# Routed attention and MLP-mixer on one core: small TensorE products regrouped within each pair of heads

## The chip, the cores and the metric

The kernel runs on one core of one Trainium2 chip. The metric is the device time of one execution in microseconds (us). The kernel before took 915.86 us, the median of 3 runs from 915.76 to 915.94. A "pair" below is two heads of one batch, which the kernel handles together. There are 4 batches of 8 heads, so 16 pairs.

## The reference

An attention whose mask comes from clusters feeds a token mixer and a channel mixer. Cut to what matters:

```python
# q, k, v: (4, 8, 768, 64) float32; centroids: (8, 16, 64)
q_assign = argmax(normalized(q) @ normalized(centroids).T)       # one of 16 clusters
k_assign = argmax(normalized(k) @ normalized(centroids).T)
mask   = q_assign[:, :, :, None] == k_assign[:, :, None, :]
scores = where(mask, q @ k.T / 8, -1e9)
attn   = exp(scores - scores.max(-1)); attn /= attn.sum(-1) + 1e-9
x      = (attn @ v) with the heads side by side                   # (4, 768, 512)
h      = relu(x.T @ w_tok1) @ w_tok2                              # 768 -> 256 -> 768
u      = x + h.T
out    = u + relu(u @ w_ch1) @ w_ch2                              # 512 -> 1536 -> 512
```

## The kernel before

For each pair `g` the kernel turns queries and keys (VectorE, tile `qkT`), multiplies them with the centroids (tile `pr`, TensorE), and takes the best cluster as a one-hot code (tiles `sim`, `mx`, `oh`, VectorE). It turns the codes on TensorE (tile `po`) and copies them out of the accumulators (PSUM) to tile `ohT`. The keys' copy is scaled so that the product of two codes is 0 in the same cluster and a huge negative number in another. This product is the mask. Scores are computed as keys by queries, one chunk of 128 keys by 384 queries (half of the queries) for two heads side by side in the array. First comes the mask in bfloat16 (`sc<-ohT`), then q times k in float32 on top of it (`sc<-qkT`). A step `m` takes three chunks, so a pair has four steps, numbered `s` = 0 to 3.

```python
    ps_w  = pool("ps_w", 1, space=PSUM)              # one bank: small products
    ps_av = pool("ps_av", 1, space=PSUM)             # one bank
    ps_sc = pool("ps_sc", NG, ps_sc_stack, space=PSUM)   # NG = 3 buffers of two banks
    ...
    work = pool("work", 7, attention)                # exponentials, tile ex
    sums = pool("sums", 2, attention)
    ...
    def scores(m):
        g, qh, j0 = split(m)                         # pair, half of the queries, first chunk
        scs = [ps_sc.tile([P, 2, 512], F32, tag="sc", name="sc") for _ in range(NG)]
        for src, start in ((st["ohT"], True), (st["T"], False)):     # masks, then products
            for i in range(NG):
                for h in range(2):
                    rows = slice(h * D, (h + 1) * D)
                    nc.tensor.matmul(
                        scs[i][:, h, 0:HS], lhsT=src[rows, 1, j0 + i], rhs=src[rows, 0, js],
                        start=start, stop=not start)
        for i in range(NG):
            ex = work.tile([P, 2, HS], F32, name="ex")
            nc.scalar.activation(out=ex, in_=scs[i][:, :, 0:HS], func=ACT.Exp, scale=SM_SCALE)

    def values(m):       # per chunk and head: av (64 x 384) += v . ex; after six chunks copied to avT
        ...
    def add_up(m):       # VectorE: the exponentials of a half added up, chunk by chunk, in tile sum
        ...
    def half_sums(hi):                               # TensorE: sum over the keys -> den
        den = st["den"] = ps_w.tile([P, 2 * HJ, QP], F32, tag="w", name="den")
        for i in range(NQ):                          # four products, each 32 columns of the array
            nc.tensor.matmul(den[rows], lhsT=ones, rhs=acc[:, :, rows], start=True, stop=True)
    def half_reciprocals(hi):                        # VectorE: den turned (dent), 1 / dent -> rcps
        ...
    def half_turn(hi):                               # TensorE: avT turned back -> px
        px = st["px"] = ps_w.tile([P, HJ, P], F32, tag="w", name="px")
        for i in range(HJ):
            nc.tensor.transpose(out=px[:, i], in_=avT[:, i], identity=ident)
    def half_out(hi):                                # VectorE: px * rcps -> x
        ...
    for m in range(last + 3):                        # last = 64 steps
        g, s = divmod(m, GROUPS)
        more = g < NPAIR - 1
        if half_at(m - 3) is not None: half_out(half_at(m - 3))
        if more and s == 0: turn(g + 1)              # VectorE
        if more and s == 1: route(g + 1)             # VectorE: sim, mx, oh
        if 1 <= m <= last: add_up(m - 1)
        if m < last: scores(m)
        ...                                          # at m == last: other PSUM pools
        if half_at(m - 2) is not None: half_sums(...); half_reciprocals(...)
        if more and s == 2: route_turn(g + 1, 1)     # po of the keys, copied by ScalarE
        if 1 <= m <= last: values(m - 1)
        if half_at(m - 2) is not None: half_turn(half_at(m - 2))
        if more and s == 0: route_products(g + 1)    # pr
        if more and s == 2: route_turn(g + 1, 0)     # po of the queries
        ...                # loads; every third step one piece of the mixers' weights is rounded
        if m >= last:
            for _ in range(3): ends.pop(0)()         # token mixer: tok1, tok2
    ...                                              # channel mixer
```

A half ends at steps `s` = 1 and 3, and its `den` and `px` come two steps later, at `s` = 3 and 1. Each engine works off its own instructions in the order in which they are issued here.

Of the kernel before, what the change touches and what calls it, by code (L numbers as in the profile page):

```python
# [18 lines left out]
P = 128  # L19
# [28 lines left out]
def kernel(  # L48
# [52 lines left out]
    loads = pool("loads", 3, attention)  # L101
    small = pool("small", 2, attention)
    qktp = pool("qktp", 2, attention)
    work = pool("work", 7, attention)
    sums = pool("sums", 2, attention)

    routing = fast.enter_context(ExitStack())
    qkpool = pool("qkpool", 2, routing, side="right")
    rsmall = pool("rsmall", 2, routing, side="right")
    pools = {}  # L110


# [3 lines left out]
    cnT = const.tile([P, H * C], F32, name="cnT")  # L116
    cnd = const.tile([P, NF, 2, C], F32, name="cnd")
    ohs = [rsmall.tile([P, 2, NJ, P], BF16, name=f"oh{i}", bufs=1) for i in range(2)]
    rcps = const.tile([P, 2 * NPAIR, 2, HJ], F32, name="rcps")
    cells = const.tile([P, NPAIR], F32, name="cells")  # L120

    W = {
# [55 lines left out]
    def weight_steps(pool, W, names):  # L178

        def tmp(name, dt, n):
            return pool.tile([P, WMAX], dt, tag=name, name=name)[:, 0:n]

        def load_bits(src, p):  # L190
            n = p["n"] = src.shape[1]
            raw = pool.tile([P, WMAX, 2], U32, tag="raw", name="raw", bufs=3)[:, 0:n]
            nc.sync.dma_start(raw.rearrange("p n two -> p (n two)"), src.bitcast(U32))
            p["lo"], p["hi"] = raw[:, :, 0], raw[:, :, 1]

        def scalar_part(p):

            p["h"] = tmp("wh", U32, p["n"])
            nc.scalar.activation(out=p["h"].bitcast(F32), in_=p["hi"].bitcast(F32), func=ACT.Abs)
            p["up"] = tmp("wup", I32, p["n"])  # L200
            nc.scalar.activation(out=p["up"], in_=p["lo"], func=ACT.Copy, scale=float(2.0**-29))

        def rest(dst, p):

            h = p["h"]
            nc.vector.tensor_scalar(
                out=h.bitcast(F32), in0=h.bitcast(F32), scalar1=TINY, scalar2=HUGE,
                op0=ALU.max, op1=ALU.min,
            )

            nc.vector.tensor_scalar(
                out=h, in0=h, scalar1=0x07FFFFFF, scalar2=3,
                op0=ALU.bitwise_and, op1=ALU.logical_shift_left,
            )
            T = tmp("wT", U32, p["n"])
            nc.vector.scalar_tensor_tensor(  # L216
                out=T, in0=p["hi"], scalar=0xC0000000, in1=h,
                op0=ALU.bitwise_and, op1=ALU.bitwise_or,
            )
            T, up = T.bitcast(I32), p["up"]  # L220
            if len(dst.shape) == 3:
                T, up = (y.rearrange("t (p j) -> t p j", j=NJ) for y in (T, up))
            nc.gpsimd.tensor_tensor(out=dst.bitcast(I32), in0=T, in1=up, op=ALU.add)  # L223

        pieces = list(weight_pieces(W, names))
        parts = [{} for _ in pieces]
        for i in range(len(pieces) + 2):

            def step(i=i):
                if 2 <= i:  # L230
                    rest(pieces[i - 2][0], parts[i - 2])
                if 1 <= i <= len(pieces):
                    scalar_part(parts[i - 1])
                if i < len(pieces):
                    load_bits(pieces[i][1], parts[i])

            yield step
# [50 lines left out]
                in_=st["qk"][:, a].rearrange("p j i d -> p (j i d)"),  # L288
            )

    def wtile(g, shape, dt, name):

        if g == 0:
            return ps_sc.tile(shape, dt, tag="sc", name=name)
        return ps_w.tile(shape, dt, tag="w", name=name)

    def route_products(g, a0=0, a1=2):

        st, f = state[g], g % NF
        pr = wtile(g, [P, a1 - a0, NJ, QP], F32, "pr")  # L300
        for i in range(NQ):
            rows = slice(i * QP, (i + 1) * QP)
            nc.tensor.matmul(  # L303
# [6 lines left out]
    def route(g, a0=0, a1=2):  # L310
# [4 lines left out]
        NR = (a1 - a0) * NJ * 2  # L315
        sc = rsmall.tile([P, NR, C], F32, name="sim")
        nc.vector.transpose(
            out=sc.rearrange("p n c -> p (n c)"), in_=st.pop("pr").rearrange("p a j r -> p (a j r)")
        )
        mx = rsmall.tile([P, NR], F32, name="mx")  # L320
        nc.vector.reduce_max(out=mx, in_=sc, axis=AX.X)
# [4 lines left out]
            op=ALU.is_ge,  # L326
        )

    def route_turn(g, a):

# [3 lines left out]
        st, oh = state[g], ohs[g % 2]  # L336
        if a == 1:
            st["ohT"] = qktp.tile([P, 2, NJ, P], BF16, name="ohT")
        po = wtile(g, [P, NJ, P], BF16, "po")
        for j in range(NJ):  # L340
            nc.tensor.transpose(out=po[:, j], in_=oh[:, a, j], identity=identb)  # L341
        if a == 0:
            if g == 0:
                nc.vector.tensor_copy(out=st["ohT"][:, 0], in_=po)  # L344
            else:
                nc.scalar.copy(out=st["ohT"][:, 0], in_=po)
        else:
            nc.scalar.activation(
                out=st["ohT"][:, 1], in_=po, func=ACT.Copy, scale=BIG, bias=-BIG,
                accum_out=cells[:, g : g + 1],  # L350
            )
# [7 lines left out]
    def scores(m):  # L359
# [1 line left out]
        st = state[g]  # L361
        js = slice(HJ * qh, HJ * qh + HJ)
        scs = [ps_sc.tile([P, 2, 512], F32, tag="sc", name="sc") for _ in range(NG)]
        for src, start in ((st["ohT"], True), (st["T"], False)):
            for i in range(NG):
                for h in range(2):
                    rows = slice(h * D, (h + 1) * D)
                    nc.tensor.matmul(  # L368
                        scs[i][:, h, 0:HS], lhsT=src[rows, 1, j0 + i], rhs=src[rows, 0, js],
                        start=start, stop=not start,  # L370
                    )
        for i in range(NG):
            ex = work.tile([P, 2, HS], F32, name="ex")
            nc.scalar.activation(out=ex, in_=scs[i][:, :, 0:HS], func=ACT.Exp, scale=SM_SCALE)  # L374
# [2 lines left out]
    def add_up(m):  # L377
# [1 line left out]
        st = state[g]  # L379
        e = [st["ex", qh, j0 + i] for i in range(NG)]  # L380
        if j0 == 0:
            acc = st["sum", qh] = sums.tile([P, 2, HS], F32, name="sum")
            nc.vector.tensor_tensor(out=acc, in0=e[0], in1=e[1], op=ALU.add)
            e = e[2:]
        acc = st["sum", qh]
        for ex in e:
            nc.vector.tensor_tensor(out=acc, in0=acc, in1=ex, op=ALU.add)  # L387

    def values(m):
# [9 lines left out]
                    start=(j == 0), stop=(j == NJ - 1),  # L399
                )  # L400
        if j0 == NJ - NG:
            st["avT", qh] = sums.tile([P, HJ, P], F32, name="avT")
            nc.scalar.copy(out=st["avT", qh].rearrange("p j t -> p (j t)"), in_=st.pop("av"))

    def half_sums(hi):

        g, qh = divmod(hi, 2)
        st = state[g]
        acc = st.pop(("sum", qh)).rearrange("p h (j t) -> p (h j) t", j=HJ)
        den = st["den"] = ps_w.tile([P, 2 * HJ, QP], F32, tag="w", name="den")  # L410
        for i in range(NQ):
            rows = slice(i * QP, (i + 1) * QP)
            nc.tensor.matmul(den[rows], lhsT=ones, rhs=acc[:, :, rows], start=True, stop=True)  # L413

    def half_reciprocals(hi):
        g, qh = divmod(hi, 2)
        dt = small.tile([P, 2 * HJ, QP], F32, name="dent")
        nc.vector.transpose(
            out=dt.rearrange("p n r -> p (n r)"),
            in_=state[g].pop("den").rearrange("p n r -> p (n r)"),  # L420
        )
        nc.vector.reciprocal(
            out=rcps[:, hi].rearrange("p h j -> p (h j)"), in_=dt[:, :, 0]
        )

    def half_turn(hi):
        g, qh = divmod(hi, 2)
        st = state[g]
        avT = st.pop(("avT", qh))
        px = st["px"] = ps_w.tile([P, HJ, P], F32, tag="w", name="px")  # L430
        for i in range(HJ):
            nc.tensor.transpose(out=px[:, i], in_=avT[:, i], identity=ident)  # L432

    def half_out(hi):

        g, qh = divmod(hi, 2)
        b, f = divmod(g, NF)
        nc.vector.tensor_tensor(  # L438
            out=xs[b][:, HJ * qh : HJ * qh + HJ, f * P : (f + 1) * P].rearrange(
                "p j (h d) -> p j h d", h=2  # L440
            ),
            in0=state[g].pop("px").rearrange("p j (h d) -> p j h d", h=2),
            in1=rcps[:, hi].rearrange("p h j -> p j h").unsqueeze(3).to_broadcast([P, HJ, 2, D]),
            op=ALU.mult,
        )
        if qh == 1:
# [224 lines left out]
    def fits():  # L671

        inside = const.tile([P, 3, 2 * NPAIR * 2 * HJ], F32, name="inside")
        good = const.tile([P, 3], F32, name="good")
        flat = rcps.rearrange("p n h j -> p (n h j)")
        for i, (limit, op) in enumerate(((LIMIT, ALU.is_le), (1.0 / LIMIT, ALU.is_ge))):
            nc.vector.tensor_scalar(
                out=inside[:, i], in0=flat, scalar1=limit, scalar2=None, op0=op
# [57 lines left out]
    begin()  # L736
    weights = list(weight_steps(stage, W, ("tok1", "tok2", "ch1")))
    last = NPAIR * GROUPS
    HALF = GROUPS // 2
    ends = [lambda t=t: tok1(0, t) for t in range(NT)]  # L740
    for b in range(B):
        if b + 1 < B:
            ends += [lambda b=b, t=t: tok1(b + 1, t) for t in range(NT)]
        ends += [lambda b=b, j=j: tok2(b, j) for j in range(NJ)]

    def half_at(m):

        return m // HALF if 0 <= m < last and m % HALF == HALF - 1 else None

    for m in range(last + 3):  # L750
        g, s = divmod(m, GROUPS)
        more = g < NPAIR - 1
        if half_at(m - 3) is not None:
            half_out(half_at(m - 3))
        if more and s == 0:
            turn(g + 1)
        if more and s == 1:
            route(g + 1)
        if 1 <= m <= last:
            add_up(m - 1)  # L760
        if m < last:
            scores(m)
        if m == last:
            ps_sc_stack.close()
            pools["ps_m"] = pool("ps_m", 2, space=PSUM)
        if half_at(m - 2) is not None:
            half_sums(half_at(m - 2))
            half_reciprocals(half_at(m - 2))
        if more and s == 2:
            route_turn(g + 1, 1)  # L770
        if 1 <= m <= last:
            values(m - 1)
        if half_at(m - 2) is not None:
            half_turn(half_at(m - 2))
        if more and s == 0:
            route_products(g + 1)
        if more and s == 2:
            route_turn(g + 1, 0)
        if s == 1 and g + 2 < NPAIR:
            load(g + 2)  # L780
        if m == last - GROUPS:
# [254 lines left out]
```

## Time and profile before

| What | Value |
|---|---|
| time, median of 3 runs | 915.86 us |
| profiled span | 914.3 us |
| VectorE busy | 507.3 us (55%) |
| ScalarE busy | 303.5 us (33%) |
| GpSimd busy | 45.0 us (5%) |
| weight loads of TensorE | 533.6 us (58%) |
| steps of the attention | first scores at 15.8 us, last `av` product begins at 365.4 us |

The attention is the first two fifths of the span; the token mixer and the channel mixer follow. In the attention the page counts each float32 product as two records of TensorE, the bfloat16 ones as one. A transpose counts as one record. Products on disjoint rows or columns of the array run side by side, so the mean duration of one record (482 ns for `sc<-qkT`) is longer than the time that passes from one to the next of the stream. Stream times are therefore read from the starts of blocks in the timeline. In the timeline a row gives the start, the time from there to the end of the last record of the block, engine and line, output and inputs, the tile of the array with the form of the operands, and the count of records. "128*32" means 128 rows by 32 columns of the array.

### The profile page before, as it was taken

To read this page: it belongs to the slowest core of one execution; us is meant where nothing else is said; L and a number is where in the kernel's file an instruction comes from. 1 tells how busy PE (TensorE), PEld (TensorE's weight loads), DVE (VectorE), ACT (ScalarE), POOL (GpSimd) and SP (SyncE) were. 2 spreads that over 40 slices of the span, in tenths; PEclk is the share of its full clock that TensorE was granted. 3 is DMA by queue.
4 is the path that set the end of the run, shared out by engine and by line. 5 is a ranking of instruction groups with operands and counts; after the bars stand their busy time and mean duration, and the time that the engine had idled before them with its cause. 6 is when DMAs were issued, how large, how long until landed. Compare 5 with 4: busy or idle time off the path is not lost.

```text
span 914.3 us, 11630 instructions
## 1 busy us (share of the span) xinstructions
PE 895.6 (98%) x4594; PEld 533.6 (58%) x4594; DVE 507.3 (55%) x851; ACT 303.5 (33%) x515; POOL 45.0 (5%) x40
## 2 busy tenths in 40 slices
PE   7999999999999999999999899999999999999997
PEld 3444444444444444444458568677686876858676
DVE  5787787787787875577463244333443334433342
ACT  2655565565565654231130121211212012130210
POOL 1000010010010100131000000000000000000000
PEclk9999999999999999999999899999999999999999
DMA  9725426325334100240000001000010000100001
GB/s 154 157 54 107 82 70 109 80 75 99 76 85 89 62 27 1 65 143 1 0 1 1 0 1 47 23 1 1 0 47 24 0 1 12 47 12 1 1 12 61
DMA packets 112830, 41.76 MB, mean 46 GB/s; under 512 B 101632, under 2 KB 105728, under 8 KB 112768
## 3 DMA queue, kind: packets, MB, share of 16 engines
q1 hardware_dynamic: 109632, 40.55, 19.4%
q10 hardware_dynamic: 3136, 0.39, 0.4%
q8 instruction: 38, 0.62, 0.3%
q14 instruction: 24, 0.20, 0.1%
HBM read 34.64 MB, written 6.29 MB: 45 GB/s over the span
## 4 chain that ended last, share of the span: by engine, by line
PE 92%; DVE 5%; DMA 1%; issue 1%; ACT 0%; DVEq 0%
PE sc L368 16%; PE pX L652 14%; PE pX L601 14%; PE av L397 13%; PE pZ L652 7%; PE pZ L601 7%; PE ph L470 5%; PE pu L479 5%; PE pY L652 3%; PE pY L601 3%; PE px L432 2%; DVE sum L387 2%; PE po L341 2%; PE den L413 1%; PE pr L303 1%; PE pt L542 1%
## 5 line engine op out<-in xcount | busy, mean ns | idle before, releaser
L374 ACT ACTIVATE ex<-sc 128x768 f32<-128x768 f32 x192 | 141.8, 812 | 117.5 <-PE sc L368 117.5
L397 PE MATMUL av<-ex,va 128*64 128x384 f32 x768 | 138.0, 494 | 0.0
L387 DVE TENSOR_TENSOR sum<-sum,ex 128x768 f32<-128x768 f32 x128 | 130.1, 1016 | 10.1
L368 PE MATMUL sc<-qkT 64*128 64x384 f32 x768 | 134.3, 482 | 0.0
L368 PEld LDWEIGHTS sc<-qkT 64*128 64x128 f32 x768 | 71.4, 187 | 38.0
L397 PEld LDWEIGHTS av<-ex,va 128*64 128x64 f32 x768 | 49.4, 136 | 66.2 <-issue 59.8
L601 PE MATMUL pX<-uT,wc 128*128 128x384 f32 x192 | 68.8, 495 | 1.6 <-issue 1.6
L609 ACT COPY p<-pX 128x384 f32<-128x384 f32 x24 | 11.4, 475 | 153.1 <-PE pX L601 153.1
L601 PEld LDWEIGHTS pX<-uT,wc 128*128 128x128 f32 x192 | 36.7, 193 | 26.7 <-issue 3.3
L223 POOL TENSOR_TENSOR wc<-wT,wup 128x512 int32<-128x512 int32 x24 | 32.4, 1349 | 251.2 <-DVE wT L216 251.2
L368 PE MATMUL sc<-ohT 64*128 64x384 bf16 x384 | 42.6, 327 | 0.6 <-DVE ohT L344 0.6
L479 PE MATMUL pu<-h,wt 128*128 128x512 f32 x96 | 42.0, 592 | 0.0
L470 PE MATMUL ph<-x,wt 128*128 128x512 f32 x96 | 42.0, 593 | 0.0
L496 DVE TENSOR_TENSOR x<-pX,x 128x256 f32<-128x256 f32 x24 | 10.2, 424 | 55.1 <-PE pX L652 55.1
L496 DVE TENSOR_TENSOR c<-pZ,u 128x384 f32<-128x384 f32 x24 | 13.4, 557 | 46.8 <-PE pZ L601 46.8
L652 PE MATMUL pX<-w2s,hA 128*128 128x256 f32 x144 | 36.4, 390 | 0.5 <-DVE x L496 0.5
L438 DVE TENSOR_TENSOR x<-px,rcps 128x384 f32<-128x384 f32 x32 | 17.8, 556 | 33.5 <-PE px L432 33.5
L496 DVE TENSOR_TENSOR hA<-pY,p 128x384 f32<-128x384 f32 x24 | 13.4, 557 | 40.4 <-PE pY L601 40.4
L652 PE MATMUL pX<-wc,hA 128*128 128x256 f32 x144 | 35.0, 379 | 0.0
L601 PE MATMUL pZ<-uTs,w1s 128*128 128x384 f32 x96 | 35.0, 487 | 0.0
L652 PE MATMUL pX<-w2s,hS 128*128 128x256 f32 x144 | 35.0, 379 | 0.0
L652 PE MATMUL pZ<-wc,hS 128*128 128x256 f32 x144 | 35.0, 379 | 0.0
(115 smaller groups left out, 1227.0 us busy)
## 6 DMA issues: line engine op xcount, KB each, us to landing
raw<-in_moe_w_ch_dram SPq DMA_DIRECT2D x24, 512.0 KB, 3.9
qk<-in_k_dram SPq DMA_DIRECT2D x64, 96.0 KB, 4.4
va<-in_v_dram SPq DMA_DIRECT2D x16, 384.0 KB, 3.3
out_dram<-x SPq DMA_DIRECT2D x24, 256.0 KB, 2.0
qk<-in_q_dram SPq DMA_DIRECT2D x60, 96.0 KB, 3.6
raw<-in_moe_w_tok_dram SPq DMA_DIRECT2D x3, 512.0 KB, 5.8
raw<-in_moe_w_tok_dram SPq DMA_DIRECT2D x4, 384.0 KB, 4.2
qk<-in_q_dram ACTq DMA_DIRECT2D x4, 96.0 KB, 4.8
```

The lines of the kernel that those rows point to most:

```text
L223: nc.gpsimd.tensor_tensor(out=dst.bitcast(I32), in0=T, in1=up, op=ALU.add)
L341: nc.tensor.transpose(out=po[:, j], in_=oh[:, a, j], identity=identb)
L368: nc.tensor.matmul(scs[i][:, h, 0:HS], lhsT=src[rows, 1, j0 + i], rhs=src[rows, 0, js], start=start, stop=not start,)
L374: nc.scalar.activation(out=ex, in_=scs[i][:, :, 0:HS], func=ACT.Exp, scale=SM_SCALE)
L387: nc.vector.tensor_tensor(out=acc, in0=acc, in1=ex, op=ALU.add)
L397: nc.tensor.matmul(st["av"][h * D : (h + 1) * D], lhsT=st["va"][:, h, j], rhs=ex[:, h], start=(j == 0), stop=(j == NJ - 1),)
L432: nc.tensor.transpose(out=px[:, i], in_=avT[:, i], identity=ident)
L470: nc.tensor.matmul(pf, lhsT=W["tok1"][:, j, t * P : (t + 1) * P], rhs=xs[b][:, j], start=(j == 0), stop=(j == NJ - 1),)
L479: nc.tensor.matmul(pu, lhsT=W["tok2"][:, t, j], rhs=h1s[b][:, t], start=(t == 0), stop=(t == NT - 1))
L496: nc.vector.tensor_tensor(out=dst, in0=a, in1=b, op=ALU.add)
L601: nc.tensor.matmul(psum, lhsT=A[a][:, k, c * P : (c + 1) * P], rhs=R[r][:, k], start=start and k == 0, stop=k == 1, skip_group_check=not s ...
L652: nc.tensor.matmul(psum, lhsT=h2[a][:, k, i * P : (i + 1) * P], rhs=Bw[w][:, 3 * part + k], start=start and k == 0, stop=k == 2, skip_grou ...
```

## The change

Three things are done to the attention loop, and buffers are moved to make room for them.

1. **Small products gathered in three places.** The sums of a pair's two halves (`den`) become one product of 384 columns per block of columns instead of two of 192, and stand with the next pair's centroid products (`pr`) after the values of step 1. They share a tile of the score pool, `den` in its first bank and `pr` in its second. Both turns of the codes (`po`) and the first half's turn back (`px`) stand after the values of step 2, the second `px` after those of step 3.
2. **The third chunk's masks behind two chunks' scores.** The new tiles take buffers of the score pool, which the third chunk of the next step takes over. Its masks are now issued after the float32 products of chunks one and two, so that there is time to read the small products out.
3. **Clusters turned ahead of use.** The copies of `ohT` are made before the pair that uses them, after step 2; that of the queries moves from ScalarE to VectorE.

For room, `work` goes from 7 buffers to 6, `rsmall` from 2 to 1, and the temporary `wT` of the weight rounding from 2 to 1; `sum` and `avT` hold a whole pair. The diff, cut to its core:

```diff
-    work = pool("work", 7, attention)
+    work = pool("work", 6, attention)
-    rsmall = pool("rsmall", 2, routing, side="right")
+    rsmall = pool("rsmall", 1, routing, side="right")
 ...
         if a == 0:
-            if g == 0: nc.vector.tensor_copy(out=st["ohT"][:, 0], in_=po)
-            else:      nc.scalar.copy(out=st["ohT"][:, 0], in_=po)
+            nc.vector.tensor_copy(out=st["ohT"][:, 0], in_=po)
 ...
-        for src, start in ((st["ohT"], True), (st["T"], False)):
-            for i in range(NG):
+        for chunks in (range(NG - 1), (NG - 1,)):
+            for src, start in ((st["ohT"], True), (st["T"], False)):
+                for i in chunks:
 ...
-    def half_sums(hi):                    # den: 192 columns, own tile in ps_w
+    def pair_sums(g, den):                # den: 384 columns, tile given
 ...
     for m in range(last + 3):
+        old = g - 1 if m < last else -1
-        if half_at(m - 3) is not None: half_out(half_at(m - 3))
-        if more and s == 1: route(g + 1)
+        if s == 2:
+            if old >= 0: pair_denominators(old)       # VectorE: dent
+            if more:     route(g + 1)                 # VectorE: sim, mx, oh
+            if old >= 0: pair_reciprocals(old)
+        if s == 3 and old >= 0: half_out(old, 0)
+        if s == 0 and old >= 1: half_out(old - 1, 1)
         if more and s == 0: turn(g + 1)
         add_up(m - 1)
         scores(m)
-        if half_at(m - 2) is not None: half_sums(...); half_reciprocals(...)
-        if more and s == 2: route_turn(g + 1, 1)
         values(m - 1)
-        if half_at(m - 2) is not None: half_turn(...)
-        if more and s == 0: route_products(g + 1)
-        if more and s == 2: route_turn(g + 1, 0)
+        if m < last and s == 1:
+            two = ps_sc.tile([P, 2, 512], F32, tag="sc", name="small")
+            if old >= 0: pair_sums(old, two[:, 0, 0:HS])
+            if more:     route_products(g + 1, pr=two[:, 1, 0:HS])
+        if m < last and s == 2:
+            if more:
+                two = ps_sc.tile([P, 2, 1024], BF16, tag="sc", name="po")
+                for a in (1, 0): route_turn(g + 1, a, ...)
+            if old >= 0: half_turn(old, 0, ps_w.tile(...))
+        if m < last and s == 3 and old >= 0:
+            half_turn(old, 1, ps_w.tile(...))
+        # m == last + 1: den, dent, reciprocals and both px of the last pair together
```

More of the change, by code (lines that the diff above doesn't have):

```diff
@@ L118 @@
     ohs = [rsmall.tile([P, 2, NJ, P], BF16, name=f"oh{i}", bufs=1) for i in range(2)]
-    rcps = const.tile([P, 2 * NPAIR, 2, HJ], F32, name="rcps")
+    rcps = const.tile([P, NPAIR, 2, 2, HJ], F32, name="rcps")
     cells = const.tile([P, NPAIR], F32, name="cells")
@@ L187, in tmp @@
         def tmp(name, dt, n):
-            return pool.tile([P, WMAX], dt, tag=name, name=name)[:, 0:n]
+            bufs = 1 if name == "wT" else 2
+            return pool.tile([P, WMAX], dt, tag=name, name=name, bufs=bufs)[:, 0:n]
         def load_bits(src, p):
@@ L289, in turn, with route_products @@
             )
[L291 to L297, printed above, removed]
+    def route_products(g, a0=0, a1=2, pr=None):
         st, f = state[g], g % NF
-        pr = wtile(g, [P, a1 - a0, NJ, QP], F32, "pr")
+        if pr is None:
+            pr = ps_sc.tile([P, (a1 - a0) * NJ * QP], F32, tag="sc", name="pr")
         for i in range(NQ):
@@ L317, in route @@
         nc.vector.transpose(
-            out=sc.rearrange("p n c -> p (n c)"), in_=st.pop("pr").rearrange("p a j r -> p (a j r)")
+            out=sc.rearrange("p n c -> p (n c)"), in_=st.pop("pr")
         )
@@ L327, in route, with route_turn @@
         )
-    def route_turn(g, a):
+    def route_turn(g, a, po=None):
         st, oh = state[g], ohs[g % 2]
@@ L338, in route_turn @@
             st["ohT"] = qktp.tile([P, 2, NJ, P], BF16, name="ohT")
-        po = wtile(g, [P, NJ, P], BF16, "po")
+        if po is None:
+            po = ps_sc.tile([P, NJ, P], BF16, tag="sc", name="po")
         for j in range(NJ):
@@ L342, in route_turn @@
         if a == 0:
[L343 to L346, printed above, removed]
+            nc.vector.tensor_copy(out=st["ohT"][:, 0], in_=po)
         else:
@@ L363, in scores @@
         scs = [ps_sc.tile([P, 2, 512], F32, tag="sc", name="sc") for _ in range(NG)]
-        for src, start in ((st["ohT"], True), (st["T"], False)):
-            for i in range(NG):
[L366 to L371, printed above, removed]
+        for chunks in (range(NG - 1), (NG - 1,)):
+            for src, start in ((st["ohT"], True), (st["T"], False)):
+                for i in chunks:
+                    for h in range(2):
+                        rows = slice(h * D, (h + 1) * D)
+                        nc.tensor.matmul(
+                            scs[i][:, h, 0:HS], lhsT=src[rows, 1, j0 + i], rhs=src[rows, 0, js],
+                            start=start, stop=not start,
+                        )
         for i in range(NG):
@@ L381, in add_up @@
         if j0 == 0:
-            acc = st["sum", qh] = sums.tile([P, 2, HS], F32, name="sum")
+            if qh == 0:
+                st["sum"] = sums.tile([P, 2, 2, HS], F32, name="sum")
+            acc = st["sum"][:, qh]
             nc.vector.tensor_tensor(out=acc, in0=e[0], in1=e[1], op=ALU.add)
             e = e[2:]
-        acc = st["sum", qh]
+        acc = st["sum"][:, qh]
         for ex in e:
@@ L401, in values @@
         if j0 == NJ - NG:
-            st["avT", qh] = sums.tile([P, HJ, P], F32, name="avT")
-            nc.scalar.copy(out=st["avT", qh].rearrange("p j t -> p (j t)"), in_=st.pop("av"))
-    def half_sums(hi):
-        g, qh = divmod(hi, 2)
+            if qh == 0:
+                st["avT"] = sums.tile([P, NJ, P], F32, name="avT")
+            js = slice(HJ * qh, HJ * qh + HJ)
+            nc.scalar.copy(out=st["avT"][:, js].rearrange("p j t -> p (j t)"), in_=st.pop("av"))
+    def pair_sums(g, den):
         st = state[g]
-        acc = st.pop(("sum", qh)).rearrange("p h (j t) -> p (h j) t", j=HJ)
-        den = st["den"] = ps_w.tile([P, 2 * HJ, QP], F32, tag="w", name="den")
+        acc = st.pop("sum").rearrange("p i h (j t) -> p (i h j) t", j=HJ)
+        st["den"] = den
         for i in range(NQ):
@@ L413, in half_sums, with pair_denominators, pair_reciprocals, half_turn @@
             nc.tensor.matmul(den[rows], lhsT=ones, rhs=acc[:, :, rows], start=True, stop=True)
[L415 to L420, printed above, removed]
-        )
[L422 to L430, printed above, removed]
-        for i in range(HJ):
-            nc.tensor.transpose(out=px[:, i], in_=avT[:, i], identity=ident)
-    def half_out(hi):
-        g, qh = divmod(hi, 2)
+    def pair_denominators(g):
+        dt = state[g]["dt"] = small.tile([P, 4 * HJ, QP], F32, name="dent", bufs=1)
+        nc.vector.transpose(out=dt.rearrange("p n r -> p (n r)"), in_=state[g].pop("den"))
+    def pair_reciprocals(g):
+        nc.vector.reciprocal(
+            out=rcps[:, g].rearrange("p i h j -> p (i h j)"), in_=state[g].pop("dt")[:, :, 0]
+        )
+    def half_turn(g, qh, px):
+        for i in range(HJ):
+            nc.tensor.transpose(
+                out=px[:, i * P : i * P + P], in_=state[g]["avT"][:, HJ * qh + i], identity=ident
+            )
+        state[g]["px", qh] = px
+    def half_out(g, qh):
         b, f = divmod(g, NF)
@@ L441, in half_out @@
             ),
-            in0=state[g].pop("px").rearrange("p j (h d) -> p j h d", h=2),
-            in1=rcps[:, hi].rearrange("p h j -> p j h").unsqueeze(3).to_broadcast([P, HJ, 2, D]),
+            in0=state[g].pop(("px", qh)).rearrange("p (j h d) -> p j h d", h=2, j=HJ),
+            in1=rcps[:, g, qh].rearrange("p h j -> p j h").unsqueeze(3).to_broadcast([P, HJ, 2, D]),
             op=ALU.mult,
@@ L674, in fits @@
         good = const.tile([P, 3], F32, name="good")
-        flat = rcps.rearrange("p n h j -> p (n h j)")
+        flat = rcps.rearrange("p n i h j -> p (n i h j)")
         for i, (limit, op) in enumerate(((LIMIT, ALU.is_le), (1.0 / LIMIT, ALU.is_ge))):
@@ L738 @@
     last = NPAIR * GROUPS
-    HALF = GROUPS // 2
     ends = [lambda t=t: tok1(0, t) for t in range(NT)]
@@ L744 @@
         ends += [lambda b=b, j=j: tok2(b, j) for j in range(NJ)]
-    def half_at(m):
-        return m // HALF if 0 <= m < last and m % HALF == HALF - 1 else None
     for m in range(last + 3):
@@ L752 @@
         more = g < NPAIR - 1
-        if half_at(m - 3) is not None:
-            half_out(half_at(m - 3))
+        old = g - 1 if m < last else -1
+        if s == 2:
+            if old >= 0:
+                pair_denominators(old)
+            if more:
+                route(g + 1)
+            if old >= 0:
+                pair_reciprocals(old)
+        if s == 3 and old >= 0:
+            half_out(old, 0)
+        if s == 0 and old >= 1:
+            half_out(old - 1, 1)
         if more and s == 0:
             turn(g + 1)
-        if more and s == 1:
-            route(g + 1)
         if 1 <= m <= last:
@@ L762 @@
             scores(m)
+        if 1 <= m <= last:
+            values(m - 1)
+        if m < last and s == 1:
+            two = ps_sc.tile([P, 2, 512], F32, tag="sc", name="small")
+            if old >= 0:
+                pair_sums(old, two[:, 0, 0:HS])
+            if more:
+                route_products(g + 1, pr=two[:, 1, 0:HS])
+        if m < last and s == 2:
+            if more:
+                two = ps_sc.tile([P, 2, 1024], BF16, tag="sc", name="po")
+                for a in (1, 0):
+                    po = two[:, a, 0 : NJ * P].rearrange("p (j t) -> p j t", j=NJ)
+                    route_turn(g + 1, a, po)
+            if old >= 0:
+                half_turn(old, 0, ps_w.tile([P, HS], F32, tag="w", name="px"))
+        if m < last and s == 3 and old >= 0:
+            half_turn(old, 1, ps_w.tile([P, HS], F32, tag="w", name="px"))
         if m == last:
@@ L765 @@
             pools["ps_m"] = pool("ps_m", 2, space=PSUM)
[L766 to L778, printed above, removed]
+            half_out(NPAIR - 2, 1)
+        if m == last + 1:
+            pair_sums(NPAIR - 1, ps_w.tile([P, HS], F32, tag="w", name="den"))
+            pair_denominators(NPAIR - 1)
+            pair_reciprocals(NPAIR - 1)
+            half_turn(NPAIR - 1, 0, ps_w.tile([P, HS], F32, tag="w", name="px"))
+            half_turn(NPAIR - 1, 1, ps_av.tile([P, HS], F32, name="av"))
+        if m == last + 2:
+            for qh in range(2):
+                half_out(NPAIR - 1, qh)
         if s == 1 and g + 2 < NPAIR:
```

## The prediction

> **What bounds the kernel now.** I read the page from the top: busy times, then the chain that ended last, then the timeline of TensorE over one pair, then the list of waits.
>
> ```profile
> span 914.3 us, 11630 instructions
> PE 895.6 (98%) x4594; PEld 533.6 (58%) x4594; DVE 507.3 (55%) x851; ACT 303.5 (33%) x515; POOL 45.0 (5%) x40
> ...
> PE 92%; DVE 5%; DMA 1%; issue 1%; ACT 0%; DVEq 0%
> ```
>
> TensorE is busy for 98% of the span and makes 92% of the chain. No other engine is near. So time is gained only where TensorE gets shorter, and the timeline must show where it is not streaming although it counts as busy. One pair, TensorE alone:
>
> ```profile
> 203.31 0.51 PE L341 MATMUL po<-identb,oh 128*128 128x128 bf16 x6
> 203.75 2.16 PE L397 MATMUL av<-ex,va 128*64 128x384 f32 x12
> 205.84 0.51 PE L341 MATMUL po<-identb,oh 128*128 128x128 bf16 x6
> 206.28 0.66 PE L368 MATMUL sc<-ohT 64*128 64x384 bf16 x6
> 206.77 2.10 PE L368 MATMUL sc<-qkT 64*128 64x384 f32 x12
> 208.80 0.53 PE L413 MATMUL den<-sum,ones 128*32 128x192 f32 x8
> 209.26 2.16 PE L397 MATMUL av<-ex,va 128*64 128x384 f32 x12
> 211.35 0.55 PE L432 MATMUL px<-ident,avT 128*128 128x128 f32 x3
> 211.83 0.66 PE L368 MATMUL sc<-ohT 64*128 64x384 bf16 x6
> 212.33 2.10 PE L368 MATMUL sc<-qkT 64*128 64x384 f32 x12
> 214.36 2.16 PE L397 MATMUL av<-ex,va 128*64 128x384 f32 x12
> 216.44 0.85 PE L303 MATMUL pr<-qkT,cnd 128*32 128x384 f32 x8
> 217.23 0.66 PE L368 MATMUL sc<-ohT 64*128 64x384 bf16 x6
> ...
> 220.22 2.16 PE L397 MATMUL av<-ex,va 128*64 128x384 f32 x12
> 222.91 0.55 PE L432 MATMUL px<-ident,avT 128*128 128x128 f32 x3 [0.54 <-DVE dent L418]
> ```
>
> Start to start, a block costs: `po` 0.44 us, `den` 0.46, `px` 0.48, `pr` 0.79, `av` 2.09, the masks 0.49, `sc<-qkT` 2.03. Now take off what the block would need if it only streamed. In the single records of the trace the next float32 pass of 384 columns starts 0.3225 us after the last, a bfloat16 mask 0.1625, a bfloat16 turn 0.056, a float32 turn 0.1085. `pr` has two passes (its four column tiles run abreast), so 0.645; `den` two of half the width, 0.3225; `po` 6 x 0.056 = 0.336; `px` 3 x 0.1085 = 0.3255. What is left is 0.14 for `pr`, 0.14 for `den`, 0.10 for `po` and 0.155 for `px`; for `av` 2.087 - 6 x 0.3225 = 0.15. That remainder appears only where the array's tile changes (128*128, 128*64, 128*32, 64*128 in the rows). Where data type changes but the tile does not, masks to `sc<-qkT`, masks take 0.497 against 3 x 0.1625 = 0.4875: 0.01, which is already their entry. So a block pays about **0.14 us** for being a separate tile layout, whatever its length.
>
> One more thing is in the last row: `px` waited. The interval from `av` to `px` is 2.69 us instead of 2.09. In the list of waits:
>
> ```profile
> PE px L432 <- DVE dent L418: 2.3, 4, 0.7
> ...
> DVE dent L418 <- PE den L413: 29.7, 15, 3.0
> ```
>
> `px` needs the one bank that `den` occupies, and VectorE comes late to read `den` when a piece of weights was rounded just before. Start to start it costs 2.0 us in the loop (three times 0.6, once 0.18), and 0.7 us behind the last pair.
>
> **What the Trainium skill says.** "TensorEngine Tiling (Array Packing)", Tiling Modes, Key Properties: changing the tiling mode, not merely the tile, drains the array. The trace agrees and gives it a size, the 0.10 to 0.155 us above. "TensorE: Matmul & The Clock Gate", Part 2, step 1: weight loads are pulled ahead of running products. The trace agrees within a layout: the float32 weight load (187 ns) shows no gap between masks and `sc<-qkT`. I rest on this for the new order of the masks. "Perfetto Trace Analysis", Tensor Engine Instruction: the end of a TensorE record is estimated. That is why I use starts only.
>
> **The change part by part.**
>
> *Gathering.* A full pair has seven small blocks now: 2 x 0.44 + 2 x 0.46 + 2 x 0.48 + 0.785 = 3.55 us. After:
> - `den` + `pr`, both 128*32 and float32: 4 passes x 0.3225 + one remainder 0.14 = 1.43.
> - `po` + `po` + `px`, all 128*128: 12 x 0.056 + 3 x 0.1085 + 0.105 = 1.10, and 0.03 for the first float32 weight load behind short turns, a guess: behind `av` the first turn of `px` takes 0.167 instead of 0.1085, so it lies between 0 and 0.06. Together 1.13.
> - `px` alone: 0.48.
>
> The sum is 3.04, or 0.51 less per pair: four layout changes fewer. The 14 pairs from the second to the fifteenth have all three places: -7.1 us.
>
> *Edges.* In the first pair `den` and `px` (0.94) fall away, and the two `po` join (0.10): -1.04. The last pair has `den` 0.785 and two `px` against two of each, 1.88: -0.14. Behind the last step the whole pair's `den` and two `px` stand instead of half a pair's. Now it is 1.23 to `px` (wait included) plus 0.36. Then: 0.35 to the last pass, 0.55 until VectorE sees it (the trace shows `sim` starting 0.554 us after the last pass of `pr`), 0.58 for a turn of 384 columns (row of `sim`, 581 ns), 0.06 to release, then six turns 0.69: 2.23. That is +0.64. Edges together: -0.54.
>
> *Wait removed.* `px` no longer follows `den` in one bank inside the loop: -2.0.
>
> *Masks moved.* Same products, same layout, two more changes of data type per step. At 0 to 0.01 us each, 64 steps cost 0 to 1.3 us. I count 0 in the centre and put it into the range.
>
> *VectorE and ScalarE.* Per pair VectorE gains one copy (558 ns, row of `ohT<-po`) and loses a reciprocal and part of a turn: 2 x 0.38 becomes 0.58, 2 x 0.19 becomes about 0.2. That is +0.2 us. Its work in the loop is near 259.65 us in 343.55 us of the window from 23.95 to 367.5, so it stays under 80% busy. ScalarE loses the copy of 0.80 us. Neither is on the path unless a buffer waits.
>
> Sum: -7.1 - 0.5 - 2.0 = -9.6. Predicted: 915.86 - 9.6 = **906.2 us**, 1.1% less. Everything behind the attention stays as it is.
>
> **The rivals.**
>
> *A new wait at the third chunk.* After `pr`, the third chunk of step 2 takes over the buffer of `den` and `pr`. Its masks begin 2 x 0.1625 + 4 x 0.3225 = 1.615 us into the step. VectorE can start the turn of `den` about 0.14 us into the step (in the built program its wait covers the whole tile, so also `pr`), then two turns of 0.58, so it is through at about 1.35 and TensorE is free at about 1.4. The slack is only 0.2 us. For it: in the kernel before, VectorE starts the turn of a pair's first `den` not 0.39 us after its last pass, as it can, but 1.0, and 2.5 where a piece of weights was due. Against it: those delays came from standing behind three additions and, when due, a piece of weights. Now VectorE's queue ahead of the turns holds two additions (1.9 us) and at most one piece (1.7), in a step of 4.6 us that begins with VectorE nearly caught up. Every 12th step a piece falls there. If a stall of 0.5 us came in each of 15 pairs, the time would be 914.
>
> *The change of data type costs.* If float32 to bfloat16 in one layout did cost like a layout change, 64 x 2 x 0.1 = 13 us would make 919. The one transition that the trace shows (bfloat16 to float32) speaks against it. The other way round is not shown.
>
> *VectorE becomes the bound.* With 6 instead of 7 buffers of exponentials, ScalarE may wait for the additions, which then delay scores. VectorE keeps above 4 us of idle time per pair, mostly waits for TensorE, so I expect none of it. It would make 908 to 912.
>
> *The gain is larger.* If `po` before `px` and `den` before `pr` hide their entries wholly, another 0.5 us goes: 905.5.
>
> **Range and chances.** The centre is a sum of starts that repeat to a hundredth of a us over the pairs, so the error lies in waits that I did not foresee, and they only add. 8 in 10: 904.8 to 909.5. A gain over 2% would need 18 us, more than all layout changes of the seven blocks in 16 pairs (16 x 7 x 0.14 = 16 us): 0.01. A loss over 2% needs the type change to cost and the third chunk to stall: 0.03.
>
> **What would show it.** In the timeline after: `den` and `pr` as neighbours, 1.43 us to the masks; `po`, `po`, `px` 1.13; a full pair near 21.5 us start to start where it was 22.0 (22.6 with the wait). The first masks of a step should take 0.33 us and the third chunk's pair 0.16. The waits should have no `px <- dent` but the last, and no TensorE wait for `sim` or `ohT` copies. The prediction is wrong if masks of the third chunk start later than 1.62 us into step 2 or 3, if the interval from `sc<-qkT` to the third masks exceeds 1.30 us in steps 0 and 1, or if exponentials wait for `sum`.

## The result and the profile after

The changed kernel took 922.08 us (median of 6 runs, 919.91 to 923.03), beside 915.68 us for the kernel before. The ratio is 1.0068, interval 1.0055 to 1.0081: it became slower by 6.4 us, where a gain of 9.6 to 906.2 us had been predicted.

The page of the changed kernel, with the engines' busy times and the chain's shares by engine:

```profile
span 921.2 us, 11319 instructions
PE 890.0 (97%) x4466; PEld 530.9 (58%) x4466; DVE 506.8 (55%) x834; ACT 295.7 (32%) x500; POOL 44.5 (5%) x40
...
PE 95%; ACT 1%; issue 1%; DMA 1%; DVE 1%
```

TensorE is busy 5.6 us less than before, and yet the span is 6.9 us longer. So TensorE now stands still somewhere. The chain says little: ScalarE appears with 1%, and one percent of the span is 9 us. The timeline of TensorE from step 1 to step 3 of one pair shows where. The columns are as before; a bracket at the end of a row gives the time for which the engine stood idle before it, and what ended that wait.

```profile
202.45 0.85 PE L412 MATMUL small<-sum,ones 128*32 128x384 f32 x8
203.12 0.83 PE L299 MATMUL small<-qkT,cnd 128*32 128x384 f32 x8
203.88 0.50 PE L364 MATMUL sc<-ohT 64*128 64x384 bf16 x4
204.21 1.45 PE L364 MATMUL sc<-qkT 64*128 64x384 f32 x8
205.50 0.33 PE L364 MATMUL sc<-ohT 64*128 64x384 bf16 x2
205.67 0.81 PE L364 MATMUL sc<-qkT 64*128 64x384 f32 x4
206.41 2.16 PE L395 MATMUL av<-ex,va 128*64 128x384 f32 x12
208.49 0.51 PE L338 MATMUL po<-identb,oh 128*128 128x128 bf16 x6
209.99 0.49 PE L338 MATMUL po<-identb,oh 128*128 128x128 bf16 x6 [0.99 <-ACT ohT L342]
210.32 0.50 PE L425 MATMUL px<-ident,avT 128*128 128x128 f32 x3
210.75 0.50 PE L364 MATMUL sc<-ohT 64*128 64x384 bf16 x4
```

Most of it came as predicted. `den` and `pr` (both now named `small`) take 203.88 - 202.45 = 1.43 us. The third chunk's masks start 205.50 - 203.88 = 1.62 us into the step. What did not come is one after the other: the second `po` begins 1.50 us after the first, in the middle of what was to be one block. The list of waits sums it up (us in total, times, longest):

```profile
PE po L338 <- ACT ohT L342: 14.8, 15, 1.0
...
PE px L425 <- DVE dent L416: 0.7, 1, 0.7
```

Fifteen waits, one in each pair that prepares a next one, are all that TensorE waits for in the loop. The old wait of `px` for `dent` is gone but for the last pair, as predicted. ScalarE's rows around the new wait:

```profile
208.61 0.48 ACT L403 COPY avT<-av 128x384 f32<-128x384 f32 x1 [1.27 <-PE av L395]
209.04 0.81 ACT L342 ACTIVATE ohT<-po 128x768 bf16<-128x768 bf16 x1
209.75 0.19 ACT L342 ACTIVATION_READ_ACCUMULATOR ohT<-po 128x1 f32 x1
```

ScalarE copies the first `po` until 209.94, and the second `po` starts 0.05 us later. Start to start the wait costs more than the 0.99 us of the list: by the bfloat16 turn of 0.056 us in the prediction, the seventh turn could have begun at 208.49 + 6 x 0.056 = 208.83, and it begins 1.16 us later. Nothing in the computation asks for that order: the two lie in different banks. But they are two halves of one tile, and the copy of the first is issued between them. My theory: the built program tracks readers and writers by the whole tile, so the second write waits for the first half's reader. The rivals: the second `po` needs the copy for another reason; the loss lies in the new order of masks, whose change of data type costs; the third chunk's buffer is waited for.

### The profile page after: what moved, and what is told of

Same layout as the page of the kernel before. It is cut to its first block, busy times and chain, and to the rows that moved or that the text cites. A ratio compares the mean times of both kernels' runs of the same rounds, so it can differ in the third digit from the quotient of the medians.

```text
span 921.2 us, 11319 instructions
## 1 busy us (share of the span) xinstructions
PE 890.0 (97%) x4466; PEld 530.9 (58%) x4466; DVE 506.8 (55%) x834; ACT 295.7 (32%) x500; POOL 44.5 (5%) x40
## 4 chain that ended last, share of the span: by engine, by line
PE 95%; ACT 1%; issue 1%; DMA 1%; DVE 1%
PE sc L364 18%; PE av L395 15%; PE pX L647 14%; PE pX L596 14%; PE pZ L647 7%; PE pZ L596 7%; PE ph L465 4%; PE pu L474 4%; PE pY L647 3%; PE pY L596 3%; PE px L425 1%; PE small L412 1%; PE pt L537 1%; PE small L299 1%; PE po L338 1%
## 5 line engine op out<-in xcount | busy, mean ns | idle before, releaser
L370 ACT ACTIVATE ex<-sc 128x768 f32<-128x768 f32 x192 | 144.6, 810 | 124.3 <-PE sc L364 79.5
L364 PE MATMUL sc<-qkT 64*128 64x384 f32 x768 | 145.0, 483 | 0.0
L385 DVE TENSOR_TENSOR sum<-sum,ex 128x768 f32<-128x768 f32 x128 | 124.4, 972 | 9.1
L364 PE MATMUL sc<-ohT 64*128 64x384 bf16 x384 | 53.3, 328 | 0.6 <-DVE ohT L340 0.6
L381 DVE TENSOR_TENSOR sum<-ex 128x768 f32<-128x768 f32 x32 | 34.7, 1083 | 1.6 <-ACT ex L370 1.6
L647 PE MATMUL pZ<-w2s,hS 128*128 128x256 f32 x144 | 35.0, 379 | 0.0
L647 PE MATMUL pY<-wc,hA 128*128 128x256 f32 x144 | 35.0, 379 | 0.0
```

The source lines that it names most:

```text
L364: nc.tensor.matmul(scs[i][:, h, 0:HS], lhsT=src[rows, 1, j0 + i], rhs=src[rows, 0, js], start=start, stop=not start,)
L647: nc.tensor.matmul(psum, lhsT=h2[a][:, k, i * P : (i + 1) * P], rhs=Bw[w][:, 3 * part + k], start=start and k == 0, stop=k == 2, skip_grou ...
```

## The experiments

Each time stands beside that of the kernel before, measured in the same session, and the ratio of the two has its 95% interval in brackets. I compare the loop as well as the time: from the first `av` of the timeline to the first product of the token mixer. It leaves out the start, which differs between runs of one kernel (last section). It was 345.63 us before and 352.99 after. In the kernel before and in `before_split_masks` the first `pr`, 0.79 us, lies ahead of this window; in the others, unless said, it lies inside.

### The turns before their copies

`turns_first` issues both `po`, then both copies:

```diff
-                for a in (1, 0):
-                    route_turn(g + 1, a, po)            # turn, then copy
+                for do in ("turn", "copy"):
+                    for a in (1, 0):
+                        route_turn(g + 1, a, po, do)
```

> The changed kernel with the twelve turns of the cluster codes of step 2 issued before both of their copies. Theory (the second po stood idle for ScalarE's copy of the first, 0.99 us, because both lie in one tile of the score pool and its copy was issued between them): that idle time goes in all 15 pairs; po to px falls from 1.83 to about 0.70 us, a pair from 22.62 to about 21.5, the time to 905 us (904 to 906.5), below both kernels, and TensorE has no wait for ohT in the loop. Rival 1 (the second po needs the copy for another reason, or the first copy only moves the wait to the third chunk): 918 to 922. Rival 2 (most of the loss is spread over scores and masks): 912 to 918.

It took 905.55 us beside 915.49, ratio 0.9884 (0.9867 to 0.9900). The loop is 335.82 us, 17.17 less than in the changed kernel. The end of the same stretch in its timeline:

```profile
220.53 0.84 PE L339 MATMUL po<-identb,oh 128*128 128x128 bf16 x12
221.21 0.50 PE L428 MATMUL px<-ident,avT 128*128 128x128 f32 x3
221.64 0.50 PE L367 MATMUL sc<-ohT 64*128 64x384 bf16 x4
```

The twelve turns are one row now. They take 0.68 us, with `px` 221.64 - 220.53 = 1.11, where it had been 2.26. Fifteen times 1.15 is 17.2 us, the whole difference of the loops. No wait of TensorE is left inside it. With two copies moved, the loss becomes the gain that had been predicted, so the rivals that place it elsewhere fall.

### The other half first

`queries_first` turns and copies in the order of the changed kernel, but the queries (VectorE copies) ahead of the keys (ScalarE copies): `for a in (0, 1)` instead of `(1, 0)`.

> The changed kernel with the queries' codes turned and copied first (by VectorE), then the keys' (by ScalarE). Theory (the wait goes to whoever reads the first half of the tile): the second po now waits for VectorE's copy of ohT, not for ScalarE's. VectorE is busy with additions until about 0.8 us after the first po begins, then copies 0.56 us, so the wait is again 0.8 to 1.0 us in each of 15 pairs and the time 918 to 923 us. Rival (ScalarE's copy or its accumulator read is special): no such wait with VectorE as the reader, 905 to 910 us.

One run took 919.96 us, with a loop of 350.50. The wait has changed its name:

```profile
PE po L338 <- DVE ohT L340: 12.3, 15, 0.8
```

Whichever engine reads the first half makes the second `po` wait. It isn't ScalarE or its accumulator. The waits are 0.17 us shorter on average, 15 times, which is the difference of the loops, 2.5 us.

### Two tiles, the old order of issue

`two_tiles` keeps the changed kernel's order, turn and copy and turn and copy, but places the second `po` in the bank of the small products and the first `px` in the bank of `av`:

```diff
-                two = ps_sc.tile([P, 2, 1024], BF16, tag="sc", name="po")
-                for a in (1, 0):
-                    route_turn(g + 1, a, two[:, a, ...])
+                route_turn(g + 1, 1)                    # own tile of the score pool
+                route_turn(g + 1, 0, ps_w.tile([P, NJ, P], BF16, tag="w", name="po"))
-                half_turn(old, 0, ps_w.tile(...))
+                half_turn(old, 0, ps_av.tile(...))
```

> The changed kernel in its own order (turn of the keys' codes, their copy, turn of the queries' codes, their copy), but the second po lies in the separate bank of the small products and the first px in the bank of av, so that the two po no longer share a tile. Theory (sharing one tile is what makes the second po wait, not the order as such and not the copy): no wait for ohT in front of the second po, 905.5 us as turns_first, within 1. Rival (the order of issue alone makes it wait): 920 us. In between, 907 to 910, if px now waits for ScalarE's copy of av.

It took 904.76 us beside 914.04, ratio 0.9905 (0.9886 to 0.9923). Its loop is 336.67 us and its turns are one row again:

```profile
219.75 0.84 PE L338 MATMUL po<-identb,oh 128*128 128x128 bf16 x12
220.43 0.51 PE L425 MATMUL av<-ident,avT 128*128 128x128 f32 x3
```

So the order alone doesn't make the wait; order and shared tile do together. The loop's 0.85 us over `turns_first` is a single wait of 0.65 us in the last pair, where `px` stands right behind `av` and needs its bank, and 0.015 us at each `px`.

### The masks alone

`before_split_masks` is the kernel before with part 2 of the change and nothing else.

> The kernel before with only the third chunk's masks moved behind the float32 products of two chunks. Theory (a change of data type within one array layout costs nothing): 915.7 us, within 0.7. Rival (it costs like a layout change, 0.1 us each way, in 64 steps): 922 to 929 us.

It took 915.43 us beside 915.49, ratio 0.9998 (0.9989 to 1.0006). The loop is 345.66 against 345.63 us. Two more changes between bfloat16 and float32 in each of 64 steps cost nothing to be seen.

### The masks in front again

`turns_first_old_masks` is `turns_first` without part 2.

> turns_first with the masks of all three chunks in front again. Theory (the third chunk takes over a buffer that VectorE and ScalarE still read): TensorE waits inside the masks, about 1.0 us for the turns of den and pr in step 2 and about 0.4 us for the copies of ohT in step 3, in 14 pairs: 905 + 20 = 925 us (918 to 930). Rival (the slack that the new order of masks gives is not needed): within 2 us of turns_first.

It took 934.71 us beside 915.49, ratio 1.0204 (1.0187 to 1.0221), and the loop is 364.72 us, 28.9 more than `turns_first`. The waits are the two that were named:

```profile
PE sc L366 <- DVE ohT L343: 13.2, 16, 1.1
PE sc L366 <- DVE sim L313: 10.6, 15, 0.7
```

Start to start, in one pair of the timeline, the third chunk's masks begin 1.24 us after the first ones in step 2 and 1.32 us in step 3, where 0.335 is enough without a wait: 0.91 and 0.98 us lost, and 15 times both is 28.4 us. The time missed the expected range because the second wait was under-sized, at 0.4 us, which fits two copies of `ohT` that run beside each other. ScalarE's and VectorE's rows show them one after the other:

```profile
217.57 0.81 ACT L345 ACTIVATE ohT<-po 128x768 bf16<-128x768 bf16 x1 [0.29 <-PE po L339]
218.28 0.19 ACT L345 ACTIVATION_READ_ACCUMULATOR ohT<-po 128x1 f32 x1
...
218.51 0.56 DVE L343 COPY ohT<-po 128x768 bf16<-128x768 bf16 x1 [1.90 <-ACT ohT L345]
```

VectorE waited for ScalarE although it reads another bank and writes another half. The two copies share two tiles: they read `po` and write `ohT`. The trace of `two_tiles`, where they still share `ohT` but no longer `po`, tells which one it is:

```profile
220.30 0.81 ACT L342 ACTIVATE ohT<-po 128x768 bf16<-128x768 bf16 x1
220.63 0.56 DVE L340 COPY ohT<-po 128x768 bf16<-128x768 bf16 x1
```

There the copies run side by side. So it is the shared `po` that holds VectorE back, although both engines only read it: the order kept within one tile holds between two readers too. In `turns_first` the copies also follow each other, but the third masks start late enough. So part 2 of the change is needed: without it the gathering loses even with the turns in front.

### A layout change by itself

`pr_apart` is `turns_first` with `pr` taken away from `den` and put in front of the values of step 1.

> turns_first with pr moved away from den, in front of the values of step 1, so that it stands alone between scores and values. The work is the same, there is one more change of the array's layout in 14 of the 16 pairs. Theory (a layout change costs 0.10 to 0.155 us whatever stands in it): 14 x 0.14 = 2.0 us more than turns_first, 907.5. Rival (gathering is worth nothing by itself, the gain came from the wait for dent that went): 905.5.

It took 906.17 us beside 914.04, ratio 0.9903 (0.9886 to 0.9919), and the loop shows 336.96 us. With the first `pr`, which here lies ahead of the window, it is 337.75, or 1.93 us more than `turns_first`. `pr` takes 0.78 us alone and `den` 0.785, so 1.57 instead of 1.43: 0.14 us for one more layout change. By the whole time alone (0.6 us between the two medians) the size could not have been told.

### Both px together, and its wait

`both_px` goes on from `turns_first`: the second `px` follows the first in step 2, in the bank of `av`, and `half_out` empties both in step 3.

> turns_first with both px behind the two po of step 2, the second one in the bank of av, which ScalarE has emptied by then; step 3 has no small product left. Theory of layout changes: one fewer in 15 pairs, 15 x 0.155 = 2.3 us less than turns_first, 903.2. Rival (the bank of av comes free too late, or VectorE empties it too late for the next values): 0.3 to 0.7 us of wait in many pairs, 905 to 912.

It took 908.29 us beside 914.04, ratio 0.9925 (0.9912 to 0.9939), and the loop 338.39 us: 2.6 more than `turns_first`. The waits of TensorE have one new line. VectorE's rows in such a pair, and TensorE's row that waited, show the cause:

```profile
PE av L398 <- DVE x L436: 4.3, 5, 0.9
```

```profile
244.87 0.56 DVE L343 COPY ohT<-po 128x768 bf16<-128x768 bf16 x1 [0.99 <-ACT ohT L345]
245.34 0.42 DVE L207 TENSOR_SCALAR wh<-wh 128x512 f32<-128x512 f32 x1
245.79 0.43 DVE L212 TENSOR_SCALAR wh<-wh 128x512 uint32<-128x512 uint32 x1
246.32 0.69 DVE L217 SCALAR_TENSOR_TENSOR wT<-raw,wh 128x512 uint32<-128x512 uint32 x1
246.93 0.55 DVE L436 TENSOR_TENSOR x<-px,rcps 128x384 f32<-128x384 f32 x1
247.40 0.55 DVE L436 TENSOR_TENSOR x<-av,rcps 128x384 f32<-128x384 f32 x1
```

```profile
248.00 1.19 PE L398 MATMUL av<-ex,va 128*64 128x384 f32 x6 [0.91 <-DVE x L436]
```

Five times, every third pair, a piece of weights (1.6 us) stands in VectorE's queue between the copy and the two products that empty the banks. The values then wait for the bank of `av`. `both_px_weights` moves just these pieces one step on; `turns_first_weights` is the control without the second `px` in step 2:

```diff
-            n = m % WEVERY == 0 or m == 1
+            n = (m % WEVERY == 0 and s != 2) or (s == 3 and (m - 1) % WEVERY == 0) or m == 1
```

> both_px with the pieces of weights that fell on step 2 (every third pair) rounded one step later. Theory (both_px loses 4.3 us because VectorE rounds a piece between the copy of ohT and the two products that empty px and the bank of av): the five waits of av for VectorE go, and the 2.3 us of the layout change stay. The loop from the first scores to the token mixer takes 339.1 us, against 343.5 in both_px and 341.4 in turns_first; the time is 903.2 us. Rival (the bank of av is too late in any case): waits of av remain, 905 us or more.

> turns_first with the same delay of the pieces of weights, as a control. Theory (the pieces cost TensorE nothing where it doesn't wait for VectorE): the loop takes 341.4 us as in turns_first, within 0.3. Rival (the delay is a gain by itself): 339 us.

`both_px_weights` took 902.95 us beside 915.51, ratio 0.9865 (0.9844 to 0.9886), the best of all. Its loop by the window used here is 333.74 us, and no wait for `x` is left. The control took 905.39 us in one run, with a loop of 335.82 us, to the hundredth that of `turns_first`. The difference, 2.08 us, is what the layout change is worth: in 14 pairs the first `px` takes 0.334 us and the second 0.423, together 0.76 instead of the 0.43 + 0.48 of two places: 0.15 us each, 2.1 in all. In the last pair, which has no `po`, the second `px` starts 0.65 us after the first instead of 0.33, since the bank of `av` is still being emptied, and what is saved there is lost again. The expectations counted the loop from the first scores, and by that count both loops are longer than expected, 340.51 and 342.49 us. The excess lies in the first step alone (last section).

## Why the prediction was wrong

**The step that failed** is the term "`po` + `po` + `px`, all 128*128 ... 1.13". It measured 2.26 us. Without the wait it measures 1.11, so the streaming part was right, and the 1.15 us came 15 times: 17.2 us. I took two neighbours in TensorE's order for one uninterrupted block and never asked what was issued between them on other engines. The timeline of the kernel before could not show this wait, because there each `po` has a tile of its own; the change put both into one. The built program has a wait for ScalarE in front of the seventh turn; I overlooked it, because I looked for waits only where a new buffer is taken, and this tile had been taken six turns earlier. The rivals followed the new buffers to the third chunk, where the prediction saw the whole-tile wait of `dent`, and missed that the same tracking holds inside step 2. Among the signs that the prediction listed, "no TensorE wait for `sim` or `ohT` copies" is the one that failed; none of the three events that it named as proof of an error came.

Point by point, what held:

- **`den` + `pr` 1.43, `px` alone 0.48**: measured 1.43 and 0.48.
- **Edges**: behind the last pair 2.27 us (1.56 to `px`, then 0.38 and 0.33), 2.23 put down.
- **Wait removed**: no `px` for `dent` in the loop.
- **Masks moved**: 0 put in the centre, 0.03 us measured.
- **Third chunk**: no stall; in the pair shown VectorE had read the small tile by 205.06, 0.44 us before the masks at 205.50, with 0.2 put down. The slack is 0.44 us in 14 of the 15 pairs and 0.91 in the first. The experiment without part 2 shows that the slack was needed.
- **VectorE as the bound**: no wait for `sum` on TensorE's path.

With that one wait taken away the kernel takes 905.55 us, where the sum had said 906.2. The loop agrees too, so this is not luck of the total: its terms add up to 10.3 us (7.1 + 1.04 + 0.14 + 2.0), and the loop of `turns_first` is 10.6 us shorter than that of the kernel before with its first `pr` (345.63 + 0.79 - 335.82).

## What to carry to other kernels

When parts of one buffer are written by one engine and read by others, issue all the writes, then all the reads, or give each part its own tile; with tiles of their own the readers need not wait for each other either. A copy issued in between can become a wait that no data asks for. After merging blocks, list the waits of the built program in front of each instruction inside the merged block, not only at its ends; a gain summed from block lengths holds only if the block really is one. And an engine far from being the bound still decides whether a bank comes free in time: look at what else stands in its queue in the worst step.

## What the runs showed of the hardware

Bfloat16 and float32 products alternate within one layout of the array at no cost (0.335 + 1.290 + 0.162 + 0.738 = 2.525 us for a step's scores, 2.526 in the old order), and bfloat16 turns pass into float32 turns of one layout just as freely: the twelve turns of `po` take 0.680 us to the start of `px`, and 12 x 0.056 is 0.672. A change of layout costs 0.14 us by undoing one of the gatherings and 0.15 us by adding one.

Less expected was the start. TensorE's granted clock, by the table of windows, was 0.54 between 15 and 19 us in the profiled run of `both_px_weights`, 0.88 in that of `turns_first` and 1.00 in that of the kernel before. In the first, eight passes of the first step took 2.56 us instead of 1.29. Where this slow stretch ends differs from one profiled run to the next, and the first scores begin between 14.4 and 15.8 us. `turns_first` and `turns_first_weights` have equal loops of 335.82 us, but these begin at 20.57 and at 21.38 us. Differences of that size between kernels are therefore read from the loop alone. Why the first stretch is at a lower clock in some runs and not in others was not tried.
